# One buffer instead of two for the gathered rows of a pair of experts

## The chip, the cores and the metric

The kernel runs on one core of a Trainium2 chip. The metric is the time of one execution on the device, in microseconds (us); the median of three runs is quoted. The profile is of one such execution. In it PE is the matmul engine (TensorE; PEld its weight loads), DVE is VectorE, ACT ScalarE, POOL GpSimd and SP SyncE. "L1144" is line 1144 of the kernel.

## What is computed

Two stages follow each other. The first is a linear recurrence over 768 time steps for 4 x 8 heads of 40 values (RWKV-7); its output is reshaped to 3072 rows (tokens) of 320 values. The second sends each row to one of 8 experts:

```python
logits = x @ w_gate
expert_idx = np.argmax(logits, axis=1)
gate_w = softmax(logits)[np.arange(N), expert_idx]
...
for e in range(E):                       # rows sorted by expert
    h = np.maximum(x_sorted[lo:hi] @ w1[e], 0.0)     # 320 -> 1024
    y_sorted[lo:hi] = h @ w2[e]                      # 1024 -> 320
return gate_w[:, None] * y_sorted[inv_perm]
```

All data are 32-bit floats.

## The kernel before

The first 511 us or so are the recurrence, computed in chunks of 64 steps, with the gate's logits and the sorting of the rows woven in. Each finished chunk writes its rows, already scaled by the gate's weight, to a table in HBM, `x_rows`: 3072 rows of 384 values, 1,536 bytes each. That part is laid out by a planner of the kernel's own (`in_order`), which also places expert 0's rows, its first layer for 384 of them and its second layer.

The second part is the loop over experts 1 to 7 at the end of the code (L1222 to L1251). There the program's text gives the dependencies, and the framework (Tile) orders each engine's instructions and puts in the waits. In the trace instructions often stand ahead of where the text has them.

An expert has room for 448 rows: three blocks of 128 and a half block of 64. The experts go in pairs: pair k holds experts 2k and 2k+1, and their two half blocks share one block of 128 rows. The steps around the change are these.

- `gathers(k)` (L1199) takes a tile `xg` of 7 x 384 values a partition from the pool `moe_x`, and issues seven indirect DMAs on POOL (L1144), each of which fetches 128 rows of `x_rows` by an index list. The order is three blocks of the first expert, the shared block, three blocks of the second.
- `turns(e)` (L1212) turns an expert's blocks with three transposes each on PE (L1152, into `tp` in PSUM), and DVE copies them into `xgT` (L1154). For an even expert it turns three blocks and the shared one; for an odd one three.
- `layer1` (L1156) multiplies by `w1`: PE (L1166 for the first 256 input values, L1174 for the last 64), with the results `hp` taken through a relu into `h_sb` by DVE (L1179) and by ACT (L1180), in turn.
- `layer2` (L1184) multiplies by `w2` (L1190, PE), ACT copies the result `zp` to `zo` (L1196), and POOL writes the rows to the output by an indirect DMA (`rows_out`, L247).
- `fetch` (L231) brings the next expert's weights, 2.6 MB, by DMAs on ACT's queue (L235, L237, L241). Where they go alternates among three places, one of which is the area `wx` that the recurrence used.

Step e of the loop does `layer1(e)`, then `turns(e+1)`, then, for an even e, `gathers` of the next pair, and then `layer2` of the three blocks. An odd e ends with the shared half blocks of its pair. Step 1 also computes expert 0's last 64 rows in `layer1`. The rows of pair 1 (experts 2 and 3) are asked for just ahead of the loop:

```python
    xgs[1] = gathers(1)
    for e in range(1, E):
...
        if e + 1 < E:
            turns(e + 1)
        if i == 0 and k + 1 < E // 2:
            xgs[k + 1] = gathers(k + 1)
```

So `gathers(2)` stands in step 2 and `gathers(3)` in step 4, each behind the turning of the odd expert's rows. The pool `moe_x` has two buffers. Pairs 1 and 3 use one of them and pair 2 the other.

The last part, for rows over 448 in an expert, is behind a branch (L1254) and takes its tile from the same pool.

Of the kernel before, what the change touches and what calls it, by code (L numbers as in the profile page):

```python
# [23 lines left out]
def kernel(  # L24
# [1111 lines left out]
    nc.vector.tensor_copy(xe[:], xe_f[:])  # L1136


    xg_pool = ctx.enter_context(tc.tile_pool(name="moe_x", bufs=2))
    wk_pool = ctx.enter_context(tc.tile_pool(name="moe_wk", bufs=3))  # L1140
    mps_pool = ctx.enter_context(tc.tile_pool(name="moe_ps", bufs=4, space=PSUM))

# [200 lines left out]
```

## Time and profile before

| what | value |
|---|---|
| median of 3 runs | 765.87 us (765.3 to 766.6) |
| profiled run | 765.49 us, span 763.7 us |
| PE busy | 720.5 us, 94% of the span |
| PE weight loads | 559.3 us, 73% |
| DVE, ACT, POOL busy | 375.4 us, 356.4 us, 296.1 us |
| mean granted PE clock | 0.98 |
| DMA | 61.07 MB, mean 80 GB/s |
| row fetches (L1144) | 21, some 0.95 us of POOL each |

Busy times are read against the span: an engine at 94% has little idle time. The page's groups name the engine, the operation, what is written and read, and at the end the idle time of the engine ahead of it and what ended most of that. "Released by PE tp" says that the instruction waited for PE to finish with the tile `tp`; "remote" that a semaphore ended the wait which the profile can't tie to an instruction; "issue" that no wait was seen. A matmul's start is recorded, its end is modelled. A DMA's row in the timeline is its issue, not its transfer. The clock column is the share of full speed that PE was granted. The DMA column is the mean busy share of the 16 DMA engines; it can come out a little over 1 in a short stretch.

### The profile page before, as it was taken

To read this page: it belongs to the slowest core of one execution; us is meant where nothing else is said; L and a number is where in the kernel's file an instruction comes from. 1 tells how busy PE (TensorE), PEld (TensorE's weight loads), DVE (VectorE), ACT (ScalarE), POOL (GpSimd) and SP (SyncE) were. 2 spreads that over 40 slices of the span, in tenths; PEclk is the share of its full clock that TensorE was granted. 3 is DMA by queue.
4 is the path that set the end of the run, shared out by engine and by line. 5 is a ranking of instruction groups with operands and counts; after the bars stand their busy time and mean duration, and the time that the engine had idled before them with its cause. 6 is when DMAs were issued, how large, how long until landed. Compare 5 with 4: busy or idle time off the path is not lost. (4 is left out here: it accounts for less than half of the span.)

```text
span 763.7 us, 35628 instructions
## 1 busy us (share of the span) xinstructions
PE 720.5 (94%) x15712; PEld 559.3 (73%) x15712; DVE 375.4 (49%) x844; ACT 356.4 (47%) x944; POOL 296.1 (39%) x472
## 2 busy tenths in 40 slices
PE   3899999899999999999999998997999999999995
PEld 2788888788888888989888886664756565564653
DVE  7577786677767767677666676411101202010110
ACT  2777666476766667776676765121011101111010
POOL 7764347233664375336742712126014020111101
PEclk9899999899999999999999999999799999999999
DMA  4433322233323323233222113319344125002000
GB/s 91 90 87 78 77 62 65 76 74 89 73 64 75 74 58 84 69 80 76 75 66 58 33 33 104 113 46 322 106 154 150 49 85 188 22 17 83 24 5 24
DMA packets 120370, 61.07 MB, mean 80 GB/s; under 512 B 100689, under 2 KB 116052, under 8 KB 120213
## 3 DMA queue, kind: packets, MB, share of 16 engines
q1 hardware_dynamic: 103176, 33.09, 17.5%
q10 hardware_dynamic: 13900, 16.23, 6.6%
q0 software_dynamic: 3136, 9.44, 3.8%
q8 instruction: 124, 2.03, 1.1%
q14 instruction: 34, 0.27, 0.1%
HBM read 50.08 MB, written 9.31 MB: 78 GB/s over the span
## 5 line engine op out<-in xcount | busy, mean ns | idle before, releaser
L513 PE MATMUL ps<-wx 64*64 64x128 f32 (+1 forms) x5376 | 150.4, 252 | 2.6 <-issue 1.5
L508 ACT COPY wx<-ps 128x512 f32<-128x512 f32 (+2 forms) x268 | 120.0, 474 | 70.4 <-PE ps L513 62.6
L513 PEld LDWEIGHTS ps<-wx 64*64 64x64 f32 x5376 | 125.8, 134 | 17.7 <-issue 6.5
L1179 DVE TENSOR_SCALAR h_sb<-hp 128x448 f32<-128x448 f32 (+1 forms) x32 | 18.3, 574 | 197.9 <-PE hp L1174 158.5
L639 DVE TENSOR_TENSOR wx<-ps,wx 64x256 f32<-64x256 f32 (+1 forms) x216 | 91.1, 422 | 35.5 <-PE ps L513 23.6
L247 POOL DMA_INDIRECT out_dram<-zo,s_idx x21 | 20.8, 988 | 160.2 <-ACT zo L1196 159.6
L574 POOL TENSOR_TENSOR KB<-KB,rv 128x512 f32<-128x512 f32 x48 | 57.3, 1212 | 42.3 <-DMA KB<-in_packed_dram 14.0
L1190 PE MATMUL zp<-w,h_sb 128*128 128x320 f32 (+1 forms) x272 | 71.0, 433 | 0.0
L1180 ACT ACTIVATE h_sb<-hp 128x448 f32<-128x448 f32 (+1 forms) x32 | 16.1, 503 | 109.1 <-PE hp L1174 43.9
L1196 ACT COPY zo<-zp 128x320 f32<-128x320 f32 x25 | 10.6, 425 | 107.8 <-PE zp L1190 99.4
L1190 PEld LDWEIGHTS zp<-w,h_sb 128*128 128x128 f32 (+1 forms) x272 | 44.4, 174 | 20.5 <-issue 1.3
L1190 PE MATMUL zp<-wx,h_sb 128*128 128x320 f32 (+1 forms) x192 | 53.6, 436 | 0.0
L603 POOL TENSOR_TENSOR GT<-GT,m_low 128x512 f32<-128x512 f32 x24 | 33.6, 1402 | 47.5 <-issue 28.4
L1166 PE MATMUL hp<-xgT,w 128*128 128x448 f32 x128 | 51.1, 547 | 0.0
L576 POOL TENSOR_TENSOR A<-A,q 128x512 f32<-128x512 f32 x24 | 28.4, 1182 | 55.1 <-DVE q L568 38.5
L702 POOL TENSOR_TENSOR TT<-TT,wx 128x512 f32<-128x512 f32 x24 | 32.6, 1357 | 30.5 <-ACT TT L508 30.5
L810 DVE TENSOR_TENSOR ZU<-ps,m_plus 128x512 f32<-128x512 f32 x48 | 30.9, 686 | 26.7 <-PE ps L513 26.6
L1190 PEld LDWEIGHTS zp<-wx,h_sb 128*128 128x128 f32 (+1 forms) x192 | 33.6, 178 | 13.2 <-issue 0.8
L508 ACT COPY T<-ps 64x256 f32<-64x256 f32 x95 | 34.8, 366 | 17.0 <-DVE wx L624 10.0
L1166 PEld LDWEIGHTS hp<-xgT,w 128*128 128x128 f32 x128 | 23.5, 190 | 25.8 <-issue 25.5
L562 DVE TENSOR_TENSOR_SCAN rv<-dec,ones 128x521 f32<-128x521 f32 x24 | 37.0, 1541 | 11.0 <-DMA dec<-in_packed_dram 9.6
L513 PE MATMUL ps<-ZU,nKB 128*64 128x104 f32 (+1 forms) x768 | 38.9, 253 | 0.2 <-issue 0.2
(243 smaller groups left out, 1344.2 us busy)
## 6 DMA issues: line engine op xcount, KB each, us to landing
KB<-in_packed_dram SPq DMA_DIRECT2D x188, 40.0 KB
w<-in_moe_w_dram ACTq DMA_DIRECT2D x16, 320.0 KB
x_rows<-xs SPq DMA_DIRECT2D x24, 192.0 KB
w<-in_moe_w_dram ACTq DMA_DIRECT2D x8, 512.0 KB
dec<-in_packed_dram SPq DMA_DIRECT2D x96, 40.0 KB
Vu<-in_packed_dram SPq DMA_DIRECT2D x96, 40.0 KB
A<-in_packed_dram SPq DMA_DIRECT2D x92, 40.0 KB
R<-in_packed_dram SPq DMA_DIRECT2D x92, 40.0 KB
```

Source lines behind the costliest of these rows:

```text
L247: ins_ = nc.gpsimd.indirect_dma_start(out=out[:, :], out_offset=bass.IndirectOffsetOnAxis(ap=si, axis=0), in_=zo, in_offset=None, bounds_c ...
L508: nc.scalar.copy(dst, src)
L513: nc.tensor.matmul(out_, lhsT=lhsT, rhs=rhs, start=start, stop=stop, skip_group_check=True)
L562: Step(pre - 0.1, DVE, 1.4, lambda e: nc.vector.tensor_tensor_scan(rv[:, : SEG * C1 + 1][:, ::-1], dec[:, ::-1], ones65[:, ::-1], 0.0, op0 ...
L574: Step(pre + 0.6, POOL, 1.2, lambda e, kb=kb, by=by: nc.gpsimd.tensor_tensor(kb, kb, by, op=ALU.mult), reads=hrv + hKB[2:], writes=hKB[q : ...
L576: Step(pre - 0.6, POOL, 1.22, lambda e: nc.gpsimd.tensor_tensor(Aq[:], Aq[:], q3[:, :, :C], op=ALU.mult), reads=hq, writes=hA)
L603: Step(rk, POOL, 1.3, lambda e, d=dst_, m=mask: nc.gpsimd.tensor_tensor(d, d, m, op=ALU.mult), writes=held)
L639: nc.vector.tensor_tensor(dst[o_, q], src[o_, q], old[o, q], op=ALU.add)
L702: Step(rk - 0.1, POOL, 1.22, lambda e, X=X, TT=TT: nc.gpsimd.tensor_tensor(TT[:], TT[:], X[:, :, :, 2, :], op=ALU.add), reads=hX[3:], writ ...
L810: Step(rk, DVE, 0.69, lambda e, s=s, ps=ps: nc.vector.tensor_tensor(ZU[:, s, :, :C], psum[:, ps.at + s, :].rearrange("x (b j) -> x b j", j=C),
L1166: nc.tensor.matmul(hps[i][:, : c1 - c0], lhsT=w[0][:, db, (fb + i) * 128 : (fb + i + 1) * 128], rhs=xT[:, db, c0:c1], start=(db == 0 and n ...
L1190: nc.tensor.matmul(zp[r0 : r0 + n], lhsT=h[:, fb, c0 : c0 + n], rhs=w[2][:, fb, :], start=(fb == 0), stop=(fb == FB - 1), skip_group_check ...
```

## The change

The pool of the gathered rows has one buffer:

```diff
-    xg_pool = ctx.enter_context(tc.tile_pool(name="moe_x", bufs=2))
+    xg_pool = ctx.enter_context(tc.tile_pool(name="moe_x", bufs=1))
```

All three pairs' rows now land in the same place, and `gathers(k+1)` can only write it when the last transposes of pair k have read it. Nothing else in the text is changed. The pool is 10,752 bytes a partition smaller, and the tiles allocated after it (`h_sb`, `xgT`, `zo`) lie that much lower.

## The prediction

> **What bounds the kernel now.** I read the busy table first: PE is busy 94% of the 763.7 us span, so only what keeps PE from working, or slows it, can move the time. Stages up to 511 us do not touch the changed buffer (its first instruction is at 515.32), so the question is the expert part, 512 to 764. The busy time by stretches, cut where each expert's first matmul starts (columns: stretch, length, then busy us and count of PE, PEld, DVE, ACT, POOL, then granted clock, DMA share, GB/s):
>
> ```profile
> 512.00:562.70 50.70, 45.15 (x188) 29.14 (x188) 5.50 (x13) 4.36 (x12) 17.16 (x18) 0.87 0.56 177
> 562.70:592.60 29.90, 29.90 (x107) 17.33 (x106) 4.08 (x7) 3.45 (x7) 9.70 (x10) 1.00 0.54 177
> 592.60:627.30 34.70, 34.70 (x141) 19.55 (x139) 4.60 (x9) 3.87 (x8) 3.93 (x4) 1.00 0.17 58
> 627.30:657.20 29.90, 29.90 (x107) 17.33 (x106) 4.08 (x7) 3.45 (x7) 2.95 (x3) 1.00 0.43 146
> 657.20:691.90 34.70, 34.70 (x141) 19.55 (x139) 4.60 (x9) 3.88 (x8) 3.93 (x4) 1.00 0.08 27
> ```
>
> From expert 2 on PE never pauses and has its full clock: 29.9 us an even expert, 34.7 an odd one. Expert 1 (first row) took 50.7 at a mean clock of 0.87. It has one thing more than experts 3 and 5, expert 0's last 64 columns: four pairs of narrow blocks, of which two took 528.01 to 530.18, so 4.35 us for four. 34.7 + 4.35 = 39.05: 11.6 us are lost there and nowhere else. The timeline of PE shows how:
>
> ```profile
> 528.01 1.00 PE L1166 MATMUL hp<-xT,w 128*128 128x64 f32 x8
> 528.94 0.66 PE L1174 MATMUL hp<-xT,w1c 64*128 64x64 f32 x6
> 529.52 0.66 PE L1166 MATMUL hp<-xT,w 128*128 128x64 f32 x4
> 535.66 0.69 PE L1174 MATMUL hp<-xT,w1c 64*128 64x64 f32 x2 [5.48 <-DVE h_sb L1179]
> ```
>
> and the timeline of all engines what DVE waited for:
>
> ```profile
> 535.38 0.36 DVE L1179 TENSOR_SCALAR h_sb<-hp 128x64 f32<-128x64 f32 x2 [8.05 <-remote]
> 535.42 0.22 ACT L1180 ACTIVATE h_sb<-hp 128x64 f32<-128x64 f32 x1 [3.81 <-remote]
> ```
>
> DVE and ACT need only PE's result here (hp), whose matmuls are shown as ended by 530.2. "Remote" says that the semaphore which freed them moved just before 535.38 with no matmul ending near it: PE's results were told 5 us late, both readers started together, and PE stood still behind them. After the gap PE ran at half clock, as the stretches around it say (same columns):
>
> ```profile
> 528.00:532.00 4.00, 2.18 (x19) 1.90 (x17) 0.00 (x0) 0.54 (x1) 3.09 (x4) 0.98 1.08 304
> 532.00:536.00 4.00, 0.34 (x2) 0.35 (x2) 0.36 (x2) 0.22 (x1) 0.61 (x1) 0.50 0.56 196
> 536.00:540.00 4.00, 4.00 (x21) 3.77 (x20) 0.15 (x1) 0.33 (x2) 0.00 (x0) 0.50 0.42 131
> 540.00:545.00 5.00, 5.00 (x20) 4.15 (x20) 1.42 (x4) 0.34 (x2) 0.00 (x0) 0.50 0.19 39
> ```
>
> What was in the air is in the DMA column: a share near 1 until 532. POOL's timeline names the rows. Pair 1's seven fetches run from 515.32; pair 2's seven follow without a pause, 84 us before their first use (turns(4), 608.4); pair 3's must wait for PE:
>
> ```profile
> 524.16 0.95 POOL L1144 DMA_INDIRECT xg<-x_rows,g_idx  x1 [0.30 <-issue]
> ...
> 531.66 0.94 POOL L1144 DMA_INDIRECT xg<-x_rows,g_idx  x1 [0.30 <-issue]
> ...
> 580.66 0.99 POOL L1144 DMA_INDIRECT xg<-x_rows,g_idx  x1 [15.62 <-PE tp L1152]
> ```
>
> The DMA queues cut at 524, 528, 532, 536 give POOL's queue (q0) 65%, 50% and 53% of 16 engines' time, against 24% in 516 to 524, when DMA was as full (weights on ACT's queue, 78%) and PE did not pause. The gap ends as pair 2's rows finish: q0 moves 0.73 MB in 532 to 536, ACT's queue 0.05.
>
> **What the Trainium skill says.** "TensorE: Matmul & The Clock Gate" (What's actually happening): PE's clock falls to 4/8 after an idle window of about 3.4 us. The trace agrees: a 5.48 us gap, then 0.50 till about 545. "Perfetto Trace Analysis", Tensor Engine Instruction: a matmul's end is an estimate, and the semaphore moves only when PSUM has acknowledged. That is why I believe the readers' 535.38 and not the 530.2. "DMA: Bandwidth & Descriptors" (Arbitration): all queues' packets share 16 engines in turn; the shares above sum to about 1. "SBUF — State Buffer" (Who interferes with whom) says that DMA never contends with a compute engine and PE never waits on anyone. Taken so, the rows could not be the cause; this trace shows PE's results late just there, so I side with the trace, but the page is my reason for not being surer.
>
> **The change part by part.**
>
> 1. *The second slot goes.* Pair 2's fetches can't go out at 524.16; they wait for the buffer's last reader, the transposes of expert 3's rows (turns(3), PE 578.7 to 580.4 now). POOL's instruction at 580.66 shows this same wait, for pair 3 in the present kernel. Removed from 524 to 536: 7 fetches, 7 x 128 rows x 1,536 B = 1.38 MB of the 6 MB that went through there. What remains is pair 1's 1.38 MB and ACT's weights; by the windows the first group is over at about 528.
>
> 2. *The gap.* If the late results are due to the second group: minus 5.48 us of gap, and the half clock goes with it. From 535.66 to 545.82 PE did half the narrow blocks, twelve transposes and two layer-2 matmuls: 10.16 us. At full clock the first cost 2.17 (528.01 to 530.18) and the rest 1.99 (the same set at expert 3, 608.43 to 610.42): 4.16. Saving 5.48 + 10.16 - 4.16 = 11.48, which agrees with the 11.6 from the stretches. Bounds: 0 if the results are late all the same; 11.6 if nothing is left; below nothing no, as there is only less traffic there. I take 10.9, leaving 0.6 for one late result of the kind seen at expert 2: its third zo copy came 13.27 us after layer 2 began (580.22 to 593.49), expert 4's 12.63.
>
> 3. *Pair 2's rows, 56 us later.* They take the place that pair 3's have now: POOL 580.66 to 589.2, 7 x 1.25 us. Their users are turns(4), at 608.4; the fourth fetch (the last needed there) is issued by 584.5, and early fetches landed 4.4 to 6.2 us after their issue, so they are there by 590.7: 17.7 us to spare. The path does not see them; expert 2's layer 2 and expert 3's layer 1 on PE hide them. Behind them on POOL are expert 2's write-backs (589.48 and 590.81, 5 us late): already so now, and PE shows no pause.
>
> 4. *Pair 3's rows, moved to expert 4*: after turns(5), PE 644.5, so POOL about 645.2 to 653.7, users at 673.0, fourth landed by 655.3: again 17.7 us. Behind them expert 4's first two write-backs (649.5, 653.8) go about 5 us late; three zo buffers and 26 us until expert 5's first zo hide that. Near them ACT fetches expert 7's weights (1.3 MB, 640.3 to 643.9), as it does expert 5's first part ahead of 580: the same company, DMA share 0.9 for 4 us, no gap. Cost 0; bounds -0 and +0.7 (a late result as at 593.5, once).
>
> 5. *SP, ACT, DVE* get no instruction more or less; all weights keep their order. The seven fetches of expert 2 and of expert 4 each gain a wait, POOL's sequencer alone: 0. The tiles behind the buffer move by 10.5 KB a partition; the first row fetch (515.32), weight load (514.60) and relu of this part start behind the last write-back of expert 0 (511.85) as one, whatever they overlap: 0, at most 0.5 either way.
>
> Sum: -10.9 + 0 = 752.8 against the profiled 763.7. The runs of before are 765.3 to 766.6 against 765.49 of the profiled one, so the profile is an ordinary run: 765.87 - 10.9 = 755.0.
>
> **The rivals.** *B, a part of the gap stays* (expert 4's first weights, 0.8 MB sent from 525 on, still crowd the first group): a gap of 2 to 3 us, with or without half clock, saves 2 to 8 us: 758 to 764. For it: results were already late at 531.07 (ACT's relu, due at 528.3). Against: no pause under the same load before 527.
>
> *C, nothing moves*: the late results come from the weights, or from DMA as such, and the change only shifts transfers that are hidden anyway: 764.4 to 767.4. For it: the skill's SBUF page. Against: 559 to 570 and 516 to 527, equally full of weights, without a gap.
>
> *D, slower*: the added wait puts rows on PE's path. Place: turns(4) at 608.4 and turns(6) at 673.0. It decides when the fourth fetch lands after those times, 17.7 us later than I reckon; if the framework queues the fetches behind expert 2's three write-backs (first at 595.2, fourth at 599, landed 605.2) only 3.2 us are left. Each us late is a us of PE idle, and past a few us half clock follows, as above about 6 us. Two places, 3 to 6 us each: 768 to 778, if the old gap stays too. For it: POOL is one queue. Against: the present kernel sends pair 3's rows ahead of those write-backs.
>
> **How the numbers follow.** A change of 0.2% (1.5 us) is about what a measurement of this kernel can tell from none. Chances: forecast A (gap and half clock gone, 753 to 757.5) 0.60; B 0.15; C 0.12; D 0.13. Faster: A, B and 0.02 of C, 0.77; same 0.10; slower 0.13. Time: 755.0, of A. The range 752.5 to 766.5 takes in A, B and nearly all of C, leaving out D and a little: about 0.84; A alone is 753 to 757.5.
>
> **What would show it.** Right: POOL's seven fetches at 515 to 524 and then none until PE's turns(3), about 570; no DVE wait of 8 us on "remote"; clock 1.00 through 528 to 545; expert 1's stretch about 39 to 40 us and every other stretch as before; fetches again about 634, none waited for by PE. Wrong: the 5 us gap at 530 with the second group gone (C), a shorter one (B), or PE's transposes waiting for xg's DMA at expert 3 or 5 (D).

## The result, and the profile after

The kernel with one buffer takes 754.85 us (752.83 to 758.38, four runs) beside 766.24 us for the kernel before: a ratio of 0.985, with a 95% interval of 0.981 to 0.990. The forecast was 755.0. The profiled run is the slowest of the four (758.38 us, span 756.7, mean granted clock 0.985; the other three have 0.991 to 0.996).

First the stretches of the kernel after, cut as before where the experts' first matmuls start (length, then busy us and count of PE, PEld, DVE, ACT, POOL, then clock, DMA share, GB/s), expert 1 and then expert 2:

```profile
512.00:555.70 43.70, 43.70 (x188) 27.83 (x188) 5.70 (x13) 4.35 (x11) 10.35 (x11) 0.92 0.55 174
555.70:585.60 29.90, 29.90 (x108) 17.36 (x107) 4.08 (x7) 3.46 (x7) 9.69 (x10) 1.00 0.54 177
```

Expert 1 takes 43.70 us in place of 50.70, and PE is busy in all of them; the experts behind it take what they took. So nearly the whole difference of the two spans, 7.0 us, lies in this stretch. The timeline of all engines, where DVE and ACT once waited 8.05 and 3.81 us for "remote":

```profile
529.23 0.23 DVE L1179 TENSOR_SCALAR h_sb<-hp 128x64 f32<-128x64 f32 x1 [2.08 <-PE hp L1174]
529.27 0.22 ACT L1180 ACTIVATE h_sb<-hp 128x64 f32<-128x64 f32 x1 [0.70 <-PE hp L1174]
```

The relus now start as their matmuls end, and the profile names the matmul as what released them. The same cuts as before around the place (same columns as above):

```profile
528.00:532.00 4.00, 4.00 (x35) 3.66 (x36) 0.45 (x2) 0.99 (x3) 0.00 (x0) 1.00 0.88 258
532.00:536.00 4.00, 4.00 (x20) 3.65 (x21) 0.56 (x3) 0.45 (x2) 0.00 (x0) 0.52 0.07 30
536.00:540.00 4.00, 4.00 (x16) 3.17 (x15) 2.19 (x5) 0.00 (x0) 0.00 (x0) 0.63 0.85 300
```

PE doesn't pause, but the clock still falls: the trace has half clock from 532.12 to 538.95, 6.83 us, where the kernel before had 13.65. POOL's timeline shows where pair 2's fetches went:

```profile
522.72 0.94 POOL L1144 DMA_INDIRECT xg<-x_rows,g_idx  x1 [0.30 <-issue]
...
573.63 0.99 POOL L1144 DMA_INDIRECT xg<-x_rows,g_idx  x1 [15.62 <-PE tp L1152]
```

Seven fetches end at 523.7, and the next begins at 573.6, held by the transposes of expert 3's rows. Pair 3's begin at 638.2. No matmul waits for either.

### The profile page after: what moved, and what is told of

Read it like the earlier page. It is cut to its first block, busy times and chain, and to the rows that moved or that the text cites. A ratio compares the mean times of both kernels' runs of the same rounds, so it can differ in the third digit from the quotient of the medians.

```text
span 756.7 us, 35629 instructions
## 1 busy us (share of the span) xinstructions
PE 719.1 (95%) x15712; PEld 557.6 (74%) x15712; DVE 375.3 (50%) x844; ACT 356.6 (47%) x944; POOL 295.5 (39%) x472
```

## The experiments

Each set of runs (1 to 4, 5 to 8, 9 to 11, and 12) shared one chip and the runs of the kernel before made there. "Stretch" is the time from expert 1's first wide matmul to expert 2's in the profiled run: a ruler that nothing outside this part of the kernel touches. "Late" is the most by which one of PE's semaphore updates in that stretch follows the end of the last matmul before it that makes such an update. The expectations of runs 1 to 4 are in us of a chip on which the kernel before takes 766; on theirs it took 760.5, so the ratio is to be read.

| run | before on that chip | ratio to before (95%) | stretch | late |
|---|---|---|---|---|
| before | 766.2 us | | 50.7 us | 5.3 us |
| after | 766.2 | 0.985 (0.981-0.990) | 43.8 | 0.05 |
| 1 same addresses | 760.5 | 0.983 (0.979-0.987) | 40.8 | 0.05 |
| 2 seven more fetches, unread | 760.5 | 0.998 (0.995-1.001) | 51.3 | 5.2 |
| 3 three buffers | 760.5 | 1.013 (1.009-1.017) | 58.4 | 12.8 |
| 4 two buffers, held back | 760.5 | 0.992 (0.988-0.995) | 43.9 | 0.05 |
| 5 seven thin fetches | 749.9 | 1.002 (0.999-1.005) | 40.8 | 0.05 |
| 6 seven plain loads on SP | 749.9 | 1.006 (1.003-1.010) | 47.3 | 0.05 |
| 7 before, weights held back | 749.9 | 1.002 (0.999-1.005) | 39.9 | 0.05 |
| 8 narrow blocks spread | 749.9 | 1.001 (0.999-1.003) | 41.2 | 0.05 |
| 9 before, again | 765.9 | 0.999 (0.996-1.002) | 50.7 | 5.4 |
| 10 as 7 | 765.9 | 0.994 (0.992-0.996) | 48.2 | 3.8 |
| 11 as 5 | 765.9 | 0.999 (0.997-1.002) | 50.9 | 5.2 |
| 12 pause between the groups | 767.3 | 0.991 (0.989-0.994) | 46.7 | 3.9 |

My theory at the start was that of the prediction: the second group's rows, as bytes in flight. The rivals: the addresses, which moved by 10.5 KB; ACT's weights; POOL's own work for a fetch, whatever it moves.

**1. The addresses.** One buffer, as large as two were:

```diff
-        xg = xg_pool.tile([128, PB, DX], F32, name="xg")
+        xg = xg_pool.tile([128, 2 * PB, DX], F32, name="xg")
```

> One buffer as in the changed kernel, but its tile is twice as long, so that every address behind it is that of the kernel before. If the time comes from the moment at which pair 2's rows are fetched: as the changed kernel, 755 us (753 to 758), no PE idle time at 530 us. If it comes from the 10.5 KB by which all later buffers moved down: as the kernel before, 765 to 767 us, with the idle time of some 5.5 us back.

It gives the whole gain (749.28 us, where the kernel before took 760.5), so the addresses do nothing. Its stretch holds no half clock:

```profile
513.90:553.30 39.40, 39.40 (x185) 24.34 (x184) 5.51 (x13) 4.34 (x11) 9.69 (x10) 1.00 0.62 192
```

With one set of instructions, in one order on every engine, the stretch takes 40.8 us here and 43.8 in the profile of the kernel after: the 3.0 us between them are a little under half of the 6.83 us of half clock.

**2. Seven fetches more.** In the kernel after:

```diff
-    xgs[1] = gathers(1)
+    scrap = scrap_pool.tile([128, PB, DX], F32, name="scrap")
+    xgs[1] = gathers(1); [gather(scrap[:, j, :], g_idx[:, 2 * PB + j : 2 * PB + j + 1]) for j in range(PB)]
```

> The changed kernel with seven more fetches, of pair 2's rows, queued on POOL straight behind pair 1's into a buffer that nobody reads; the fetches that the layers use stay where the change put them. If rows of a second pair in flight at 524 to 536 us are what made PE's results late: 765 to 767 us, PE idle for some 5 us near 530 us, although nothing waits for these rows by a semaphore. If what counts is the order of the fetches that are used (their waits, their buffer): 755 us, no idle time.

```profile
534.31 0.68 PE L1174 MATMUL hp<-xT,w1c 64*128 64x64 f32 x2 [5.38 <-DVE h_sb L1179]
```

The idle time is back, though no instruction reads these rows. It is the second group of fetches in its old place that matters, and no wait on it. What in the group, this run leaves open.

**3. Three buffers**, `bufs=3` in the pool of the kernel before, so that 21 fetches leave in a row.

> The kernel before with three buffers, so that 21 fetches go out in a row from 515 us. If fetches in flight make PE's results late: as the kernel before or worse, 766 to 775 us, with PE's idle time beginning near 530 us and perhaps a second one about 540 us. If the second pair's fetches hurt by something special to them (their place behind the first seven): 766 us and no further idle time.

```profile
542.87 0.68 PE L1174 MATMUL hp<-xT,w1c 64*128 64x64 f32 x2 [13.10 <-issue]
```

Not two pauses but one of 13.1 us, until POOL's run of fetches is over (541.0). More buffers, more loss.

**4. Two buffers, held back.** The kernel before, with the next pair's fetches queued behind the write-backs of the pair before:

```diff
-            xgs[k + 1] = gathers(k + 1)
+            with tc.issue_after(last_out): xgs[k + 1] = gathers(k + 1)
```

> Two buffers as in the kernel before, but each pair's fetches are held back until the last write-back of the pair before has been issued, as the one buffer holds them, and by no buffer. If the hour of the fetches counts: 753 to 758 us. If the one buffer itself counts (addresses, its wait on the turns): 765 to 767 us.

```profile
557.60 0.99 POOL L1144 DMA_INDIRECT xg<-x_rows,g_idx  x1 [0.30 <-issue]
...
559.28 0.62 DVE L1179 TENSOR_SCALAR h_sb<-hp 128x448 f32<-128x448 f32 x1 [20.76 <-PE hp L1174]
```

754.59 us: no late result and no idle time, with two buffers, so the hour of the fetches is enough to remove both. The fetches run from 557.6 to 566.1 us here, beside expert 2's wide first layer, and its relus still start within 0.04 us of their matmuls' ends. In time about half of run 1's gain is there: the ratio is 0.992, and 753 to 758 of 766 us would be 0.983 to 0.990. The medians of runs 1 and 4 are 5.3 us apart (0.9%). Run 4's profile has the 6.83 us of half clock of the kernel after, again without a pause, and its stretch is 3.1 us longer than run 1's. So that the single buffer adds nothing of its own isn't shown.

**5 to 8, a chip without the idle time.** Here the kernel before took 749.9 us, and none of four kernels was faster. The kernel before has no profile on this chip, nor was the kernel after timed on it; run 7, the kernel before but for the hour of some weights, has no late result and no idle time in its trace. Two of them were put on another chip later (10 and 11), and are told there.

> The changed kernel with the same seven further fetches on POOL as in the run with the echo, as many instructions and rows, but 64 bytes a row in place of 1,536: 57 KB instead of 1.38 MB. If it is the bytes in flight that make PE's results late: the time of the changed kernel (ratio to before 0.980 to 0.990), no idle time of PE near 530 us. If it is POOL's own work for a fetch (its instructions, 896 row descriptors): the time of the kernel before (ratio 0.997 to 1.003), with some 5 us of idle PE.

> The kernel before, both groups of fetches in their old place, but expert 4's first weights on ACT's queue (two of 128 KB and two of 512 KB, sent at 525 to 536 us) held back until expert 1's first zo copy at about 548 us. If the weights are what makes PE's results late, or are needed for it beside the rows: no idle time or a much shorter one, ratio 0.983 to 0.993. If the rows do it alone: PE idle for 3 to 5 us near 530, ratio 0.995 to 1.003.

The thin fetches on this chip, at the usual cuts:

```profile
528.00:532.00 4.00, 4.00 (x25) 2.96 (x23) 1.07 (x3) 0.77 (x2) 2.88 (x4) 1.00 1.02 274
532.00:536.00 4.00, 4.00 (x34) 3.71 (x34) 0.45 (x2) 0.65 (x3) 1.83 (x2) 1.00 0.55 165
```

POOL works on fetches (2.88 us of 4), DMA is full, and PE has no gap and its full clock. A change that removes the idle time can gain nothing where there is none: 5, 7 and 8 are within 0.2% of the kernel before. As tests they decide nothing.

Run 6 moved the same bytes by SP's queue:

```diff
+            if extra and fb == 4: tc.keep_in_program_order(nc.vector.memset(scrap[:, :, 0:1], 0.0)); [nc.sync.dma_start(scrap[:, j, :], x_d[j * 128 : (j + 1) * 128, :]) for j in range(PB)]
```

> The changed kernel with seven plain loads of 128 rows by 1,536 B on SP's queue, begun at about 525 us, where the kernel before began the second pair's fetches: the same bytes, in packets of the same size, but without POOL. If bytes in flight are what counts, by whichever queue: as the kernel before, ratio 0.995 to 1.005, PE idle for about 5 us near 530. If it takes POOL's queue: as the changed kernel, ratio 0.980 to 0.990.

```profile
530.31 0.35 ACTq L235 DMA_DIRECT2D wx<-in_moe_w_dram  x1
530.71 0.54 ACT L1180 ACTIVATE h_sb<-hp 128x448 f32<-128x448 f32 x1 [8.19 <-DMA scrap<-x_rows]
...
531.30 1.97 PE L1166 MATMUL hp<-xT,w 128*128 128x64 f32 x8 [2.37 <-ACT h_sb L1180]
```

PE was idle for 2.4 us, but for a reason of its own: no PE result is late. ACT's relu stood behind ACT's next weight load, which waited for one of the new loads to land. That is my edit's own wait, and so the run says nothing on bytes.

Run 8 put expert 0's narrow blocks between expert 1's wide ones, in the kernel after:

```diff
-        layer1(w, xTs[e], h, 0, CAP, parts[: FB // 2])
...
-            layer1(weights[0], xTs[0], hs[0], MAIN, CAP, parts)
...
+        for fb in range(0, FB, 2) if e == 1 else ():
+            layer1(w, xTs[e], h, 0, CAP, parts[0::2] + parts[1::2], [fb])
+            layer1(weights[0], xTs[0], hs[0], MAIN, CAP, (), [fb])
```

> The changed kernel with expert 0's narrow blocks of 64 columns put between expert 1's wide ones, one pair after each. In the profile of the changed kernel half clock stood from 532.1 to 538.9 us with PE busy throughout, just behind a row of narrow blocks. If that row of narrow blocks brings the half clock: full clock from 512 to 555 us, expert 1's stretch at 39 to 40 us, and a time 2 to 4 us under the changed kernel's (ratio to before 0.976 to 0.984). If the half clock has another cause (the transposes, the row fetches): 0.982 to 0.990, the half clock still there.

It has its full clock, but so have runs 5 and 7 with the narrow blocks in a row. Neither a gain nor the cause of the half clock is shown.

**9 to 11, one more chip, with a profile of the kernel before.**

> The kernel before once more, unchanged, with a profile of its own: in the last set of runs it took 749.9 us, 16 us less than in the first, with the changed kernel's kin no faster. If its idle time near 530 us comes and goes with the chip: either a time of 758 us or more with PE's results 5 us late and the idle time there, or one of some 750 us with PE busy from 512 to 555 us. If the idle time is in the program and something else was faster: the idle time also at 750 us.

```profile
538.23 0.69 PE L1174 MATMUL hp<-xT,w1c 64*128 64x64 f32 x2 [5.54 <-DVE h_sb L1179]
```

762.68 us, with the idle time of the first profile to within 0.1 us. It comes and goes with the chip (or with the hour, as each chip had one set of runs): four of the five sets of runs have it, in a trace or in the time of the kernel before, and the one of runs 5 to 8 has not.

Run 11, the kernel after with seven fetches of 64 bytes a row:

```diff
-            out=xg, out_offset=None, in_=x_d[:, :], in_offset=bass.IndirectOffsetOnAxis(ap=gi, axis=0),
+            out=xg, out_offset=None, in_=x_d.rearrange("n (a b) -> (n a) b", b=xg.shape[-1]), in_offset=bass.IndirectOffsetOnAxis(ap=gi, axis=0),
...
+    scrap = scrap_pool.tile([128, PB, 16], F32, name="scrap")
+    xgs[1] = gathers(1); [gather(scrap[:, j, :], g_idx[:, 2 * PB + j : 2 * PB + j + 1]) for j in range(PB)]
```

> The changed kernel with seven further fetches of 64 bytes a row on POOL, again, beside a profile of the kernel before on the same chip. Where that one shows PE's late results: if bytes in flight bring them, none here, ratio 0.980 to 0.990; if POOL's work for a fetch does, some 5 us of idle PE and a ratio of 0.997 to 1.003. Where that one shows none: ratio 0.998 to 1.004 under both, nothing told.

```profile
534.80 0.94 POOL L1144 DMA_INDIRECT scrap<-x_rows,g_idx  x1 [0.30 <-issue]
...
538.45 0.36 DVE L1179 TENSOR_SCALAR h_sb<-hp 128x64 f32<-128x64 f32 x2 [7.95 <-remote]
...
538.73 0.69 PE L1174 MATMUL hp<-xT,w1c 64*128 64x64 f32 x2 [5.38 <-DVE h_sb L1179]
```

This is the deciding run. 57 KB do what 1.38 MB did: the same "remote" wait of 8 us, the same idle time, a ratio of 0.999. A fetch costs POOL the same 0.94 us for 64 bytes a row as for 1,536. So my theory falls: it is not the bytes of the second group that hold PE's results, but something that goes with the number of its fetches. That may be POOL's own work for a fetch, the 128 rows of each as separate packets, or their landings (the arrivals of the data, which semaphores tell); this run changes none of the three. It leaves the weights and the first group's rows in flight, too. The Trainium skill, "DMA: Bandwidth & Descriptors" (SWDGE vs HWDGE vs iDMA), says that for a DMA issued from GpSimd software computes the descriptors; a cost that doesn't go with the bytes agrees with that.

Run 10, the kernel before with expert 4's first weights held back by the same `tc.issue_after`, behind expert 1's first zo copy on ACT:

> The kernel before with expert 4's first weights held back to about 548 us, again, beside a profile of the kernel before on the same chip. Where that one shows PE's late results: if the rows alone bring them, idle time of 3 to 5 us here too, ratio 0.995 to 1.003; if the weights are needed for it beside the rows, none or little, ratio 0.983 to 0.993. Where that one shows none: ratio 0.998 to 1.004 under both, nothing told.

```profile
533.44 0.36 DVE L1179 TENSOR_SCALAR h_sb<-hp 128x64 f32<-128x64 f32 x2 [7.79 <-remote]
...
533.72 1.97 PE L1166 MATMUL hp<-xT,w 128*128 128x64 f32 x8 [3.88 <-DVE h_sb L1179]
```

With these weights gone (the DMA share of 532 to 536 falls to 0.09) PE still stands for 3.9 us, of 5.5. The ratio, 0.994, is just under what I gave for "the rows alone". The weights are not needed for the effect. That they make it longer isn't clean: in this kernel the order of PE's transposes changed too. No run took the rows' bytes and the weights away together.

**12. A pause.** The kernel before, with a memset and four additions on POOL (5.0 us) ahead of pair 2's fetches:

```diff
-    xgs[1] = gathers(1)
+    xgs[1] = gathers(1); pauses = [tc.keep_in_program_order(nc.gpsimd.memset(scrap[:], 0.0))] + [tc.keep_in_program_order(nc.gpsimd.tensor_tensor(scrap[:], scrap[:], scrap[:], op=ALU.add)) for _ in range(4)]
...
+            with tc.issue_after(pauses[-1].ins): xgs[k + 1] = gathers(k + 1)
```

> The kernel before, with other work on POOL (a memset and four additions of 128x512, at 1.2 us each as such additions take in the recurrence, some 5 us together) between pair 1's seven fetches and pair 2's seven, which then run from about 529 to 538 us, beside the narrow blocks and what follows them. If it takes 14 fetches in a row to hold PE's results: no results 2 us late or more, no idle time of PE between 512 and 556 us, ratio to before 0.980 to 0.992. If any seven hold them that run beside the narrow blocks: results 3 to 6 us late, idle time of 3 to 6 us that ends 2 to 3 us after the last fetch, ratio 0.995 to 1.005. On a chip on which the kernel before takes some 750 us: ratio 0.997 to 1.003 under both, nothing told.

```profile
535.78 0.23 DVE L1179 TENSOR_SCALAR h_sb<-hp 128x64 f32<-128x64 f32 x1 [2.87 <-PE hp L1166]
...
539.03 0.94 POOL L1144 DMA_INDIRECT xg<-x_rows,g_idx  x1 [0.30 <-issue]
...
541.53 1.02 DVE L1154 COPY xgT<-tp 128x384 f32<-128x384 f32 x2 [2.65 <-remote]
542.15 1.54 PE L1152 MATMUL tp<-ident,xg 128*128 128x128 f32 x6 [3.97 <-DVE xgT L1154]
```

Fourteen without a break are not needed: with 5 us of other work between the groups the second still holds results, and the idle time (3.97 us) moves with it: counted from expert 1's first matmul, from 18.1-23.6 us to 23.6-27.6. It now falls on the transposes. The narrow blocks ran beside the first four fetches of the second group with their relus on time (the third pair's at 535.78, of four); the first result over 0.1 us late is the relu of 538.66. During POOL's memset and additions no result was late either. The ratio lies in the range of the other theory, since the idle time is 1.5 us shorter and only 3.4 us of half clock followed where the kernel before has 13.65.

## Why the prediction was right, and where not

**Step 1** held: seven fetches from 515.2 to 523.7, the next at 573.6 (I said about 570).

**Step 2** had the event right and its cause wrong. The 5.48 us of idle time went, as it said. But it charged them to "1.38 MB of the 6 MB that went through there" (by the trace 3.5 MB went through from 524 to 536; 6 MB is what went from 516 on). Run 11 refutes that with 57 KB. In its place the traces show a tie to POOL's run of fetches: the results that PE then stood for come 1.5 to 2.8 us after the run's last fetch has ended on POOL, in all seven traces that have them, from at least three chips. They are, as end of the fetch and release: 532.6 and 535.4 (before), 531.4 and 534.0 (run 2), 541.0 and 542.6 (3), 535.1 and 537.9 (9), 531.0 and 533.4 (10), 535.7 and 538.4 (11), 540.0 and 541.5 (12). The tie to the landings is as near: in each of the seven a landing of that last fetch is recorded within 0.8 us of the release (run 12: release 541.51, landings from 541.58). By what path the fetches hold up PE's semaphore, no run shows.

Step 2's other half, "and the half clock goes with it", is right only in part. The stretch fell from 50.7 us to 40.8 where no half clock stayed (run 1) and to 43.8 where 6.83 us of it did; the stretch check had said 39.05. So the term of 10.9 measures 9.9 at best and 6.9 in the profiled run. Part of that is a sum of mine. I took the narrow blocks as half done ahead of the gap, but the lines shown have 18 of their 48 matmuls there (8, 6 and 4) and so 30 behind it. Run 1 does the work that I had put at 4.16 us, from the same matmul on and at full clock, in 5.8 us:

```profile
530.09 0.43 PE L1174 MATMUL hp<-xT,w1c 64*128 64x64 f32 x2
...
535.91 10.39 PE L1190 MATMUL zp<-wx,h_sb 128*128 128x320 f32 x38
```

With 5.82 in place of 4.16 the saving comes to 9.8, beside the 9.9 of run 1; the stretches had the same error, and their agreement with 11.48 was no support. The interval of the ratio, 0.981 to 0.990, is 7.9 to 15 us and takes in 9.9; that the median met 755.0 owes something to luck. I had also written that the trace agrees with an idle window of about 3.4 us ahead of the half clock. It doesn't: in the kernel before half clock begins at 531.81, when PE has stood for 1.6 us, and PE was busy for 1.8 of the 3.41 us ahead. Why half clock came without idle time in the kernel after and in run 4, and not in run 1 with the same order of instructions, stays open.

The skill's "SBUF — State Buffer" (Who interferes with whom) made me less sure. Its word on DMA and engines fits run 11: the amount of data made no difference. That PE never waits on anyone is said there of SBUF's ports. The wait in these traces is another one: PE's results were told up to 12.8 us late (run 3), and PE stood still for the engines that read them. So the page was an argument neither for nor against.

**Steps 3 and 4** held. The fetches run at 573.6 and 638.2, the fourth of pair 2 is issued by 578.4, and PE waits for no row. The late result allowed for at expert 2 is there, 0.65 us at 586.39, and costs nothing. Why the new place is safe is not shown. It is not that PE goes on there without late results: the first two of expert 2's layer 2 come within 0.1 us of their matmuls' ends while the fetches run (577.13 and 581.51). Nor are wide or narrow blocks unsafe beside fetches as such, by run 4 and by the first four fetches of run 12's second group. In the loop over the experts, results over 1 us late were seen only during or just behind a group of fetches that followed another within some 5 us; seven alone held nothing up by more than 0.7 us in any trace.

**Step 5** held: run 1 puts the addresses back and keeps the gain.

**The rivals.** C, "DMA as such", is refuted by run 11 for the rows' bytes and by run 10 for the weights, each taken alone; its outcome, that nothing moves, is what the kin of the changed kernel showed on the chip of runs 5 to 8. B, that the weights still crowd the first group, did not happen. D's row wait didn't either. The rival that the runs leave, a cost of each fetch apart from its bytes, was not on my list, nor was the chip.

## What to carry to other kernels

Fetching earlier than needed is not free, even when nobody waits for the data: here a second run of seven row fetches on POOL, close behind a first, held up the matmul engine's results, and the same seven 50 us later cost nothing. When a consumer's wait is marked "remote", line its end up with what other queues were doing, and then vary the bytes and the number of transfers separately before blaming either. Measure such a gain on more than one chip: here it was 1.5% on one, and on another three kernels much like it gained nothing.

## What the runs showed of the hardware

The chips differ in how many landings of fetches the trace records. A DMA of POOL that lands alone shows 16 semaphore updates (run 12, 541.6). With the thin fetches POOL issues 63 DMAs, which makes 1,008 such updates; the trace has 998 of them on the chip without idle time and 610 on the other; from 524 to 536 us, 184 and 22. On that first chip no PE result is over 0.05 us late in the stretch. On the chips with idle time updates go missing already in the first group, while the relus still start on time (524.24 in the kernel before, marked "issue"); PE's results come late only in the second. A missing record is not the delay itself: the kernel after and run 1 have 660 and 667 of 896, and no late result in the stretch. What sets the two groups apart is not settled. From its second fetch on, each fetch of the second group waits for the semaphore of an earlier one, which the first group's don't; a run without these waits was not made. Every timed run lists a granted clock, so it was recorded as well: whether the delay would be there in an execution that nobody records, these runs can't tell.

TensorE's half clock came in windows of 3.41 us or a multiple of it, in every trace, but for the one that the end of the kernel cuts off. Twice (the kernel after and run 4) it came behind a window in which PE was busy throughout with narrow blocks, and in run 1 the same blocks kept full clock.
